# Second MLP of a fused attention, MLP, MLP kernel: three passes of four feature blocks in place of three sweeps over all twelve

## The chip, the cores and the metric

The kernel runs on one core of a Trainium2 chip. The metric is the device time of one execution in microseconds (us). Engines are named as in the profile: PE is TensorE (PEld its weight loads), DVE is VectorE, ACT is ScalarE, POOL is GpSimd, SP is SyncE, which here issues every DMA from one queue, in order.

## What is computed

Three stages follow each other: windowed attention on four batches of 576 tokens and eight heads, a first MLP that takes the maximum of three projections, and a second, gated MLP. The change touches the third alone. Cut to what matters:

```python
# second MLP: x is 2304 x 512, w_gate and w_val 512 x 1536, w_out 1536 x 512
g = x @ w_gate
silu = g * (1.0 / (1.0 + np.exp(-g)))
val = x @ w_val
out = (silu * val @ w_out).astype(np.float32)
```

## The kernel before

**Precision.** The weights arrive as 64-bit floats, which the chip reads as pairs of 32-bit integers. `single` (L91) turns such a pair into one float: a scaled copy on ACT (L96) and three integer instructions on DVE (L99, L100, L102). Every operand of a product is then split into a rounded head and a rest by `split` (L106): the head is an ACT copy (L107), the rest a subtraction (`low`, L85) on the engine that the caller names. A product is three matmuls: head by head, head by rest, rest by head.

**Tiles of the second MLP.** Tokens go in PAIRS = 3 pairs of blocks of HT = 384 tokens, called c. Features go in NF2 = 12 blocks of 128, called f. For each (c, f) the gate and value products of the pair of token blocks are computed together by a seven-product scheme (`PRODUCTS`, L31) in the manner of Strassen and Winograd: seven products of one combination of token blocks (A11, S2, A12, S3, S1, A22, S4) with one combination of weights (B11, T2, B21, T3, T1, T4, B22), where a plain computation takes eight. Each product is 2 x 3 matmuls of 384 columns.

**Preparing the weights of a block.** `prep(f)` (L510) has four pieces: `first` and `second_` load the gate and value weights, convert them with `single` and split them; `mixed` forms T1 to T4 by four DVE subtractions (L534) and splits the two tiles; `down_w` does the same to the rows of `w_out`. The rests of these five splits are on POOL. Every finished tile is also stored to `w_dram` (`store`, L507).

**The loops.** One step n is one (c, f), f inner: all 12 blocks for token pair 0, then for pair 1, then for pair 2. For c = 0 the weights are made by `prep`, AHEAD = 4 blocks ahead of their use; for c = 1 and 2 they are read back from `w_dram` by `load_w` (L553), five DMAs a block. The weight tiles live in two sets of buffers: 18 for the up side (tag "w"), 6 for the down side (tag "wo"). Token tiles are made by `tokens_steps(c)` (L590): four loads from `y_dram`, where the first MLP left its output, sums on DVE (L587), and 14 tiles split by ACT and DVE. They have 14 buffers, and for c = 1 and 2 four tiles use free weight buffers.

**A step.** `head(n)` (L636) issues products 1 and 6 of step n, and products 4 and 3 of step n - 1 with what follows them; `tail(n)` (L663) issues products 2, 7 and 5. ACT copies the first product (L641, the tile `s`) and takes two sigmoids (L653, L669); DVE does nine sums and products of 384 columns (L629, L657, L659, L660, L670). `act` (L631) rounds the two results on POOL (L88) and takes their rests on POOL (L85). The product accumulates in PSUM banks "a", "b" and "c", which DVE reads between products: PE can't go on to product 7 in bank "b" before DVE has read product 6 from it.

**The down product.** `down(c, g, t)` (L681) multiplies GROUP = 3 feature blocks for 128 tokens t (six of these to a token pair): 9 matmuls of 512 columns. The first group of a pair is copied to an accumulator by ACT (L694), the other three groups are added to it by DVE (L629, `acc`); the last one is stored to `out`. These come LAG = 4 steps behind, two to a step, as filler between the products.

**Order.** The framework lists each engine's instructions in an order that it plans at build time; engines then run in order and wait on semaphores. The vector work of a step has a priority of 100 over the rest (`HIGH`). Before the loop, the token tiles of pair 0 and the weights of blocks 0 to 3 are made beside the end of the first MLP.

Of the kernel before, what the change touches and what calls it, by code (L numbers as in the profile page):

```python
# [8 lines left out]
F32 = mybir.dt.float32  # L9
# [26 lines left out]
GROUP, LAG, AHEAD = 3, 4, 4  # L36
# [18 lines left out]
def kernel(ctx: ExitStack, tc, q0, k0, q1, k1, qk0, qk1, vv, w123, wo1, wgv, wo2, out):  # L55
# [26 lines left out]
    w_dram = dram.tile([NF2, 5, P, 2, 512], F32, name="w_dram")  # L82
# [414 lines left out]
    def second(apool, raws2, ps_o):  # L497
# [3 lines left out]

        def weight_tile(name, out=False):
            if out:
                return down_tile(name)
            return up_tile(name)

        def store(f, i, n=512):  # L507
            nc.sync.dma_start(out=w_dram[f, i, :, :, :n], in_=ws[0, f][i][:, :, :n].bitcast(F32))

        def prep(f):  # L510

            t = ws[0, f] = {}
            sums, ab = {}, {}
# [5 lines left out]
            def first():  # L519
                load(0)  # L520
                t[0] = weight_tile(f"u{f}_0")
                split(t[0], ab[0], nc.gpsimd)
                store(f, 0)

            def second_():
                load(1)
                t[3] = weight_tile(f"u{f}_3")
                split(t[3][:, :, :256], ab[1][:, 256:], nc.gpsimd)
                store(f, 3, 256)

            def mixed():
                tt = raws2.tile([P, 2, 512], F32, tag="sum", name="tt", bufs=1)
                b11, b21, b12, b22 = ab[0][:, :256], ab[0][:, 256:], ab[1][:, :256], ab[1][:, 256:]
                low_ = lambda o, x, y: nc.vector.tensor_tensor(out=o, in0=x, in1=y, op=ALU.subtract)  # L534
                t1, t3, t2, t4 = tt[:, 0, :256], tt[:, 0, 256:], tt[:, 1, :256], tt[:, 1, 256:]
                low_(t1, b12, b11)
                low_(t3, b22, b12)
                low_(t2, b22, t1)
                low_(t4, b21, t2)
                for i in (1, 2):  # L540
                    t[i] = weight_tile(f"u{f}_{i}")
                    split(t[i], tt[:, i - 1], nc.gpsimd)
                    store(f, i)

            def down_w():
                load(2)
                t[4] = weight_tile(f"u{f}_4", out=True)
                split(t[4], ab[2], nc.gpsimd)
                store(f, 4)

            return [first, second_, mixed, down_w]
# [16 lines left out]
        def tokens(c, name):  # L568

            x = raw_y[name]  # L570
            parts = blocks[c, name] = []
            for k in range(2):
                if (c, name) in {(1, "A11"), (1, "S2"), (2, "A12"), (2, "S3")}:
                    t = wpool.tile([P, 2, HT], F32R, tag="w", name="ya", bufs=3 * NF1)
# [15 lines left out]
        def tokens_steps(c):  # L590
# [7 lines left out]
            def four():  # L598
# [3 lines left out]
            rest = [lambda n=n: tokens(c, n) for n in ("S3", "S1", "A22", "S4")]  # L602
            return [lambda: load_y(c), one, lambda: tokens(c, "S2"), four] + rest

        def product(n, m, bank, first):

            c, f = divmod(n, NF2)
# [8 lines left out]
            w = ws[c, f][i]  # L616
            for k in range(2):
                y = blocks[c, a][k]
                wh, wl = [w[:, x, col + k * P:col + k * P + P] for x in range(2)]
# [5 lines left out]
        def scratch(tag):  # L625
            return temp.tile([P, HT], F32, tag=tag, name=tag)
# [3 lines left out]

        def act(n, i, h):  # L631
            t = acts[n, i] = actp.tile([P, 2, HT], F32R, tag="act", name="act")
            pool_round(t[:, 0], h)
            low(nc.gpsimd, t[:, 1], h, t[:, 0])

        def head(n):  # L636
            if n < PAIRS * NF2:
                p1 = product(n, 1, "a", True)
                with tc.high_priority(HIGH):
                    s1 = scratch("s1")  # L640
                    nc.scalar.copy(s1, p1)  # L641
                p6 = product(n, 6, "b", True)
                with tc.high_priority(HIGH):
                    u2 = scratch("u2")
                    add(u2, p6, s1)
                late[n] = s1, u2
            if n:
                s1, u2, u3, h0 = late.pop(n - 1)
                p4 = product(n - 1, 4, "b", False)
                with tc.high_priority(HIGH):  # L650
                    add(s1, p4, s1)
                    h1 = scratch("h1")
                    nc.scalar.activation(out=h1, in_=s1, func=AF.Sigmoid)  # L653
                p3 = product(n - 1, 3, "c", False)
                with tc.high_priority(HIGH):
                    add(u2, p3, u2)
                    nc.vector.tensor_tensor(out=h0, in0=h0, in1=u2, op=ALU.mult)  # L657
                    act(n - 1, 0, h0)
                    nc.vector.tensor_tensor(out=h1, in0=s1, in1=h1, op=ALU.mult)  # L659
                    nc.vector.tensor_tensor(out=h1, in0=u3, in1=h1, op=ALU.mult)  # L660
                    act(n - 1, 1, h1)

        def tail(n, piece):  # L663
# [3 lines left out]
            with tc.high_priority(HIGH):  # L667
                h0 = scratch("h0")
                nc.scalar.activation(out=h0, in_=p2, func=AF.Sigmoid)  # L669
                nc.vector.tensor_tensor(out=h0, in0=p2, in1=h0, op=ALU.mult)  # L670
            piece()
            p7 = product(n, 7, "b", False)
            with tc.high_priority(HIGH):
                u3 = scratch("u3")
# [6 lines left out]
        def down(c, g, t):  # L681

            po = ps_o.tile([P, 512], F32, tag="o", name="po", bufs=2)
            i, tt = divmod(t, HT // P)
            for f in range(g * GROUP, (g + 1) * GROUP):
                ah, al = [acts[c * NF2 + f, i][:, x, tt * P:tt * P + P] for x in range(2)]
                w = ws[c, f][4]
                nc.tensor.matmul(po, ah, w[:, 0], start=f == g * GROUP, stop=False)  # L688
                nc.tensor.matmul(po, ah, w[:, 1], start=False, stop=False)  # L689
                nc.tensor.matmul(po, al, w[:, 0], start=False, stop=f == (g + 1) * GROUP - 1)  # L690
            with tc.high_priority(HIGH):
                if g == 0:
                    acc[c, t] = accp.tile([P, 512], F32, tag="acc", name="acc")
                    nc.scalar.copy(acc[c, t], po)  # L694
                else:
                    add(acc[c, t], po, acc[c, t])
            if (g + 1) * GROUP == NF2:
                r0 = 2 * c * HT + t * P
                nc.sync.dma_start(out=out[r0:r0 + P, :], in_=acc.pop((c, t)))

        return prep, load_w, tokens_steps, head, tail, down


# [31 lines left out]
    apool = en("apool", 14, reuse_waits="tile")  # L735
    ps_o = en("ps_o", space=PSUM, reuse_waits="tile")
    prep, load_w, tokens_steps, head, tail, down = second(apool, raws2, ps_o)

    conv = tokens_steps(0) + [piece for f in range(AHEAD) for piece in prep(f)]
    spread(down_groups(*order[-2]) + up_groups(*order[-1]), conv[:16])  # L740
    spread(down_groups(*order[-1]), conv[16:])
    mctx.close()
    actp, accp, temp = em("actp", 10), em("accp", 7), em("temp", 2)
    ctx.enter_context(mctx)

    downs = []
    for n in range(PAIRS * NF2 + 1):
        c, f = divmod(n, NF2)
        others = []
        m = n + AHEAD  # L750
        if m < NF2:
# [85 lines left out]
```

## Time and profile before

| | before |
|---|---|
| median of 3 runs | 915.24 us (914.71 to 917.12) |
| the profiled execution, its own time | 913.06 us |
| its span, first to last instruction | 911.4 us |
| PE busy in the span | 867.0 us (95%) |
| DVE busy | 654.4 us (72%) |
| POOL busy | 484.1 us (53%) |
| ACT busy | 394.8 us (43%) |
| DMA queue of SP: packets' time as a share of 16 engines | 50.1% |

Shares of the whole span mix three stages with different limits. Matmuls are pipelined, so that their durations overlap: a busy PE says that it was never empty, and its rate is read from the distance between like instructions. The granted clock of PE is given as a share of its higher level.

### The profile page before, as it was taken

The numbers are of one execution on the slowest core, as the hardware profiler recorded it, in microseconds if no ns is written. First come the engines' busy times: TensorE is split into PE (matmuls) and PEld (weight loads), VectorE is DVE, ScalarE is ACT, GpSimd is POOL, SyncE is SP. The second block draws the span as 40 slices with busy tenths as digits, with TensorE's granted clock in tenths as the row PEclk, the third lists the DMA queues.
The fourth block names the chain that finished last, engine by engine and source line by source line (L and its number), as shares of the span: only waits on it lengthen the run. The fifth ranks groups of instructions, "written<-read, shape, count | busy, mean of one in ns | idle before, by whom it ended". The sixth has DMA issues, their size and how long they took to land.

```text
span 911.4 us, 16010 instructions
## 1 busy us (share of the span) xinstructions
PE 867.0 (95%) x5352; PEld 797.5 (88%) x5352; DVE 654.4 (72%) x1593; ACT 394.8 (43%) x1110; POOL 484.1 (53%) x675
## 2 busy tenths in 40 slices
PE   8999999999999999998787978899999999999997
PEld 5687889999999999998686867789999999999996
DVE  7998936676676757569699999999744566644553
ACT  6977658665575647243443433333121122121110
POOL 5586776767776675626547674752422231422221
PEclk9999999999999999999989999999999999999999
DMA  9842523233121411135786566789856673766401
GB/s 332 298 126 79 165 84 117 59 111 102 53 85 57 122 62 54 47 116 198 291 302 218 205 236 203 268 317 367 309 175 231 218 256 129 270 213 227 149 7 70
DMA packets 65138, 157.81 MB, mean 173 GB/s; under 512 B 6432, under 2 KB 26912, under 8 KB 65056
## 3 DMA queue, kind: packets, MB, share of 16 engines
q1 hardware_dynamic: 65056, 156.79, 50.1%
q8 instruction: 43, 0.70, 0.3%
q14 instruction: 39, 0.32, 0.1%
HBM read 119.01 MB, written 37.75 MB: 172 GB/s over the span
## 4 chain that ended last, share of the span: by engine, by line
PE 73%; DVE 17%; issue 3%; POOL 3%; DMA 3%; ACT 1%; SPq 0%; DVEq 0%; POOLq 0%; ACTq 0%
PE ps L124 10%; PE ps L122 10%; PE ps L123 10%; PE pg L620 5%; PE pg L622 5%; PE pg L621 5%; PE po L690 4%; PE po L688 4%; PE po L689 4%; DVE wf L100 3%; DVE wr L102 3%; DVE tt L534 3%; PE pv L400 2%; DMA wr<-wgv 2%; PE pc L620 2%
## 5 line engine op out<-in xcount | busy, mean ns | idle before, releaser
L122 PE MATMUL ps<-x,w 128*128 128x320 f32 (+1 forms) x576 | 172.0, 302 | 1.3 <-DVE m L165 1.0
L124 PE MATMUL ps<-x,w 128*128 128x320 f32 (+1 forms) x576 | 172.1, 300 | 0.1
L123 PE MATMUL ps<-x,w 128*128 128x320 f32 (+1 forms) x576 | 171.8, 299 | 0.0
L88 POOL TENSOR_SCALAR act<-h 128x384 fp32r<-128x384 f32 x72 | 45.3, 635 | 208.7 <-DVE h L657 201.0
L620 PE MATMUL pg<-ya,u 128*128 128x384 f32 x360 | 125.0, 349 | 20.6 <-DVE u L629 9.6
L621 PE MATMUL pg<-ya,u 128*128 128x384 f32 x360 | 123.2, 342 | 0.0
L622 PE MATMUL pg<-ya,u 128*128 128x384 f32 x360 | 123.1, 343 | 0.0
L122 PEld LDWEIGHTS ps<-x,w 128*128 128x128 f32 x576 | 107.9, 188 | 4.2 <-DVE m L165 1.3
L124 PEld LDWEIGHTS ps<-x,w 128*128 128x128 f32 x576 | 108.5, 188 | 2.6 <-DVE w L85 1.1
L123 PEld LDWEIGHTS ps<-x,w 128*128 128x128 f32 x576 | 108.5, 188 | 1.2 <-issue 0.9
L372 POOL TENSOR_SCALAR_AFFINE_SELECT t<-pk 128x512 fp32r<-128x512 f32 (+3 forms) x128 | 76.4, 619 | 49.9 <-PE pv L400 26.0
L620 PEld LDWEIGHTS pg<-ya,u 128*128 128x128 f32 x360 | 69.2, 192 | 31.7 <-DVE u L629 13.5
L688 PE MATMUL po<-u,act 128*128 128x512 f32 x216 | 86.9, 402 | 0.5 <-DVE acc L629 0.5
L689 PE MATMUL po<-u,act 128*128 128x512 f32 x216 | 86.3, 399 | 0.0
L690 PE MATMUL po<-u,act 128*128 128x512 f32 x216 | 85.5, 400 | 0.5 <-POOL act L85 0.5
L85 POOL TENSOR_TENSOR act<-h,act 128x384 fp32r<-128x384 f32 x72 | 82.3, 1150 | 3.2
L621 PEld LDWEIGHTS pg<-ya,u 128*128 128x128 f32 x360 | 69.3, 192 | 3.5
L324 ACT ACTIVATE z<-z,mn 128x128 f32<-128x128 f32 (+1 forms) x160 | 63.4, 398 | 20.3 <-DVE mn L319 19.4
L622 PEld LDWEIGHTS pg<-ya,u 128*128 128x128 f32 x360 | 69.2, 192 | 1.1 <-POOL u L85 0.8
L629 DVE TENSOR_TENSOR u<-pg,s 128x384 f32<-128x384 f32 x72 | 39.4, 551 | 41.8 <-PE pg L622 41.8
L85 POOL TENSOR_TENSOR u<-wr,u 128x512 fp32r<-128x512 f32 (+1 forms) x36 | 47.1, 1312 | 37.4 <-ACT u L107 37.4
L165 DVE TENSOR_TENSOR m<-ps,m 128x256 f32<-128x256 f32 (+1 forms) x96 | 43.2, 452 | 30.4 <-PE ps L124 27.1
(116 smaller groups left out, 2197.9 us busy)
## 6 DMA issues: line engine op xcount, KB each, us to landing
u<-w_dram SPq DMA_DIRECT2D x96, 512.0 KB, 5.3
w_dram<-u SPq DMA_DIRECT2D x48, 512.0 KB, 5.5
wr<-wgv SPq DMA_DIRECT2D x24, 512.0 KB, 5.2
qkr<-qk SPq DMA_DIRECT2D x24, 416.0 KB, 3.6
wr<-w SPq DMA_DIRECT2D x18, 512.0 KB, 6.0
wr<-wo SPq DMA_DIRECT2D x12, 512.0 KB, 5.9
u<-w_dram SPq DMA_DIRECT2D x24, 256.0 KB, 4.3
yr<-y_dram SPq DMA_DIRECT2D x12, 384.0 KB, 3.8
```

The costliest lines, as they stand in the source:

```text
L85: eng.tensor_tensor(out=out, in0=raw, in1=head.bitcast(F32), op=ALU.subtract)
L122: nc.tensor.matmul(ps, wh, xt_h, start=first, stop=False)
L123: nc.tensor.matmul(ps, wh, xt_l, start=False, stop=False)
L124: nc.tensor.matmul(ps, wl, xt_h, start=False, stop=last)
L324: nc.scalar.activation(out=z[:m, a], in_=z[:m, a], func=AF.Exp, scale=-1.0, bias=mn[:m, a:a + 1], accum_out=sm[:m, a:a + 1],)
L372: nc.gpsimd.affine_select(out=t[:, i, :n, :, :m], in_=w[:, :n, :, :m], compare_op=op, fill=0.0, base=0, pattern=[[0, n], [0, 2], [-sign, m ...
L620: nc.tensor.matmul(o, wh, y[:, 0], start=first and k == 0, stop=False, skip_group_check=True)
L621: nc.tensor.matmul(o, wh, y[:, 1], start=False, stop=False, skip_group_check=True)
L622: nc.tensor.matmul(o, wl, y[:, 0], start=False, stop=k == 1, skip_group_check=True)
L688: nc.tensor.matmul(po, ah, w[:, 0], start=f == g * GROUP, stop=False)
L689: nc.tensor.matmul(po, ah, w[:, 1], start=False, stop=False)
L690: nc.tensor.matmul(po, al, w[:, 0], start=False, stop=f == (g + 1) * GROUP - 1)
```

## The change

The loops are turned: the 12 feature blocks go in NPASS = 3 passes of PASS = 4. In a pass all three token pairs are worked through with the pass's four blocks, so that each weight tile is made once and stays in SBUF; `w_dram`, `store` and `load_w` are gone. Pairs run 0, 1, 2, then 2, 1, 0, then 0, 1, 2. A run of four steps with one pair in one pass is a segment; there are nine.

What goes through DRAM instead: in pass 0 each split token tile is stored to `a_dram` when it is made (3 x 14 tiles of 384 KB), and in passes 1 and 2 `tokens_again` loads the 14 tiles at each change of the pair, four times in all. The partial outputs of passes 0 and 1 are stored to `o_dram` (18 tiles of 256 KB in each pass) and loaded again in passes 1 and 2. Token tiles have 14 + EXTRA = 17 buffers.

The rests of the up weights' splits move from POOL to DVE, so that of five only that of `outs` stays on POOL. The rounding in `act` moves from POOL to ACT. The values' half tile is shared by an even and an odd block, so that four blocks take 14 up tiles in place of 16.

The down product takes four blocks at once, in two halves of 6 matmuls, three halves to a step, one segment behind. Only passes 1 and 2 add on DVE: 36 times in place of 54. Of the weights of blocks 0 to 3 the last two pieces move into step 0; blocks 4 to 7 are made in steps 4 to 12 and blocks 8 to 11 in steps 16 to 24, three pieces a step.

```diff
-GROUP, LAG, AHEAD = 3, 4, 4
+PASS = 4
+NPASS = NF2 // PASS
+SEGMENTS = [(p, c) for p in range(NPASS) for c in (range(PAIRS) if p % 2 == 0 else range(PAIRS - 1, -1, -1))]
+EXTRA = 3
...
-    w_dram = dram.tile([NF2, 5, P, 2, 512], F32, name="w_dram")
+    a_dram = dram.tile([PAIRS, 14, P, 2 * HT], F32, name="a_dram")
+    o_dram = dram.tile([NT, DM], F32, name="o_dram")
...
-                split(t[0], ab[0], nc.gpsimd)
-                store(f, 0)
+                split(t[0], ab[0], nc.vector)
...
+                both = up_tile(f"u{f}_3") if f % 2 == 0 else ws[f - 1][5]
+                t[3], t[5] = both[:, :, f % 2 * 256:f % 2 * 256 + 256], both
+                split(t[3], ab[1][:, 256:], nc.vector)
...
-                    split(t[i], tt[:, i - 1], nc.gpsimd)
-                    store(f, i)
+                    t[i] = up_tile(f"u{f}_{i}")
+                    split(t[i], tt[:, i - 1], nc.vector)
...
-        def load_w(c, f):
-
-            t = ws[c, f] = {}
-            for i, n in ((0, 512), (2, 512), (1, 512), (3, 256), (4, 512)):
-                t[i] = weight_tile(f"u{f}_{i}", out=i == 4)
-                nc.sync.dma_start(out=t[i][:, :, :n].bitcast(F32), in_=w_dram[f, i, :, :, :n])
...
+                t = apool[made[0] % (14 + EXTRA) // 14].tile([P, 2, HT], F32R, tag="a", name="ya")
+                made[0] += 1
+                kept = a_dram[c, 2 * names.index(name) + k].rearrange("p (a n) -> p a n", a=2)
+                if load:
+                    nc.sync.dma_start(out=t.bitcast(F32), in_=kept)
                 else:
-                    t = apool.tile([P, 2, HT], F32R, tag="a", name="ya")
-                split(t, x[:, k], nc.vector)
+                    split(t, raw_y[name][:, k], nc.vector)
+                    nc.sync.dma_start(out=kept, in_=t.bitcast(F32))
...
-            pool_round(t[:, 0], h)
-            low(nc.gpsimd, t[:, 1], h, t[:, 0])
+            split(t, h, nc.gpsimd)
...
+            if half == 0:
+                ps["o"] = ps_o.tile([P, 512], F32, tag="o", name="po", bufs=2)
+                o = acc[t] = accp.tile([P, 512], F32, tag="acc", name="acc")
+                if p:
+                    nc.sync.dma_start(out=o, in_=o_dram[r0:r0 + P, :])
+            po = ps["o"]
+            for j in range(2 * half, 2 * half + 2):
+                ah, al = [acts[g * PASS + j, i][:, x, tt * P:tt * P + P] for x in range(2)]
+                w = ws[p * PASS + j][4]
...
+            if half:
+                o = acc.pop(t)
+                with tc.high_priority(HIGH):
+                    if p:
+                        add(o, po, o)
+                    else:
+                        nc.scalar.copy(o, po)
+                nc.sync.dma_start(out=(out if p == NPASS - 1 else o_dram)[r0:r0 + P, :], in_=o)
...
+        if p + 1 < NPASS:
+            for q, when in enumerate((4, 9, 10, 11)):
+                if at == when:
+                    conv += prep((p + 1) * PASS + q)
+        if j == 0:
+            ahead = []
+            if g + 1 < len(SEGMENTS) and SEGMENTS[g + 1][1] != c:
+                p1, c1 = SEGMENTS[g + 1]
+                ahead = tokens_steps(c1) if p1 == 0 else tokens_again(c1)
```

## Rows read from the trace of the kernel before

**Rows 1.** Table by stretch: length; busy PE, PEld, DVE, ACT, POOL (count); PEclk, DMA, GB/s.
```profile
443.80:454.50 10.70, 6.83 (x36) 6.19 (x36) 5.54 (x6) 5.18 (x10) 6.55 (x5) 1.00 0.99 368
454.50:500.60 46.10, 37.55 (x170) 32.81 (x170) 44.16 (x70) 20.32 (x37) 27.22 (x23) 0.89 0.73 261
500.60:552.80 52.20, 43.59 (x203) 38.11 (x204) 50.12 (x71) 21.49 (x41) 35.50 (x31) 0.94 0.63 223
552.80:614.70 61.90, 54.53 (x252) 47.26 (x251) 61.76 (x93) 20.88 (x40) 37.37 (x33) 0.94 0.76 265
614.70:657.40 42.70, 42.70 (x227) 40.14 (x226) 38.63 (x64) 11.75 (x27) 15.25 (x18) 1.00 0.92 337
657.40:888.40 231.00, 231.00 (x1201) 214.32 (x1200) 122.13 (x221) 41.67 (x82) 66.87 (x82) 1.00 0.55 190
888.40:911.40 23.00, 18.38 (x79) 14.00 (x77) 7.86 (x13) 0.53 (x1) 3.09 (x4) 1.00 0.19 69
```

**Rows 2.** Timeline of ACT: a step's first copy, of steps 0 and 1, 16, and 35.
```profile
454.54 0.84 ACT L641 COPY s<-pg 128x384 f32<-128x384 f32 x2
...
657.37 0.48 ACT L641 COPY s<-pg 128x384 f32<-128x384 f32 x1 [2.82 <-PE pg L622]
...
876.61 0.48 ACT L641 COPY s<-pg 128x384 f32<-128x384 f32 x1 [4.70 <-PE pg L622]
```

**Rows 3.** Waits from 448 to 600 us: us in total, times, longest.
```profile
PE pg L620 <- DVE u L629: 9.6, 6, 3.2
PE pc L620 <- DVE u L629: 8.2, 6, 2.5
```

**Rows 4.** DVE's groups by shape from 448 to 600 us: count | busy us, mean ns.
```profile
L102 DVE SCALAR_TENSOR_TENSOR wr<-wr,wf 128x512 int32<-128x512 int32 x27 | 27.5, 1019 | 0.5
L100 DVE SCALAR_TENSOR_TENSOR wf<-wr,wf 128x512 int32<-128x512 int32 x27 | 25.7, 951 | 0.2
L99 DVE TENSOR_SCALAR wf<-wf 128x512 int32<-128x512 int32 x27 | 18.0, 667 | 4.7 <-ACT wf L96 4.7
L534 DVE TENSOR_TENSOR tt<-wr,tt 128x256 f32<-128x256 f32 x18 | 13.6, 756 | 0.0
L534 DVE TENSOR_TENSOR tt<-wr 128x256 f32<-128x256 f32 x18 | 11.1, 655 | 0.0
```

**Rows 5.** Durations over the whole trace by line: least/median/most ns, first and last start.
```profile
L629 DVE TENSOR_TENSOR u<-pg,s x72: 539/550/560, 457.3 to 886.1; 128x384 f32<-128x384 f32 x72
L102 DVE SCALAR_TENSOR_TENSOR wr<-wr,wf x66: 404/684/1786, 14.6 to 601.7; 128x512 int32<-128x512 int32 x54, 128x256 int32<-128x256 int32 x12
L99 DVE TENSOR_SCALAR wf<-wf x66: 280/428/1532, 12.5 to 596.1; 128x512 int32<-128x512 int32 x54, 128x256 int32<-128x256 int32 x12
L85 DVE TENSOR_TENSOR w<-wr,w x18: 664/682/1216, 17.1 to 83.5; 128x512 fp32r<-128x512 f32 x18
L85 POOL TENSOR_TENSOR act<-h,act x72: 1002/1115/1588, 480.4 to 897.5; 128x384 fp32r<-128x384 f32 x72
```

**Rows 6.** Timelines of DVE and of POOL at one moment: start us, us.
```profile
498.92 1.62 DVE L659 TENSOR_TENSOR h<-s,h 128x384 f32<-128x384 f32 x1
500.46 0.54 DVE L629 TENSOR_TENSOR u<-pc,u 128x384 f32<-128x384 f32 x1
...
498.54 1.58 POOL L85 TENSOR_TENSOR u<-tt,u 128x512 fp32r<-128x512 f32 x1
```

**Rows 7.** POOL's groups by shape from 448 to 600 us: count | busy us, mean ns.
```profile
L85 POOL TENSOR_TENSOR u<-wr,u 128x512 fp32r<-128x512 f32 x19 | 28.5, 1503 | 16.3 <-ACT u L107 16.3
L85 POOL TENSOR_TENSOR u<-tt,u 128x512 fp32r<-128x512 f32 x18 | 25.2, 1402 | 19.6 <-ACT u L107 19.4
```

**Rows 8.** Waits of SP's DMA queue over the span: us in total, times, longest.
```profile
SPq L508 <- POOL u L85: 112.9, 45, 7.9
```

**Rows 9.** Table by stretch again, around the first change of token pair.
```profile
603.00:645.00 42.00, 42.00 (x221) 39.17 (x220) 40.74 (x65) 13.04 (x30) 17.15 (x17) 1.00 1.01 374
```

**Rows 10.** DMA issues: count, KB each, median us from issue to landing.
```profile
yr<-y_dram SPq DMA_DIRECT2D x12, 384.0 KB, 3.8
```

More of the change, by code (lines that the diff above doesn't have):

```diff
@@ L500, in second @@
         made = [0]
[L502 to L508, printed above, removed]
+        names = ("A11", "S2", "A12", "S3", "S1", "A22", "S4")
         def prep(f):
[L512 to L513 removed]
+            t = ws[f] = {}
+            ab = {}
             def load(i):
@@ L679, in tail, with down @@
             late[n] = s1, u2, u3, h0
-        def down(c, g, t):
-            po = ps_o.tile([P, 512], F32, tag="o", name="po", bufs=2)
+        def down(g, t, half):
+            p, c = SEGMENTS[g]
+            r0 = 2 * c * HT + t * P
             i, tt = divmod(t, HT // P)
[L685 to L688, printed above, removed]
-                nc.tensor.matmul(po, ah, w[:, 1], start=False, stop=False)
[L690 to L699, printed above, removed]
@@ L734 @@
     raws2 = en("raws2", RAWS, reuse_waits="tile")
-    apool = en("apool", 14, reuse_waits="tile")
+    apool = [en("apool", 14, reuse_waits="tile")]
     ps_o = en("ps_o", space=PSUM, reuse_waits="tile")
[L737 to L741, printed above, removed]
+    STEPS = [(c, p * PASS + j) for p, c in SEGMENTS for j in range(PASS)]
@@ L742 @@
+    prep, tokens_steps, tokens_again, head, middle, tail, down = second(apool, raws2, ps_o)
+    conv = tokens_steps(0) + [piece for f in range(PASS) for piece in prep(f)]
+    spread(down_groups(*order[-2]) + up_groups(*order[-1]), conv[:18])
+    spread(down_groups(*order[-1]), conv[18:22])
+    conv = conv[22:]
     mctx.close()
-    actp, accp, temp = em("actp", 10), em("accp", 7), em("temp", 2)
+    actp, accp, temp = em("actp", 10), em("accp", 4), em("temp")
+    apool.append(en("apool2", EXTRA, reuse_waits="tile"))
@@ L744 @@
     ctx.enter_context(mctx)
[L746 to L751, printed above, removed]
[L752 to L761 removed]
+    downs, ahead = [], []
@@ new lines @@
+    for n, (c, f) in enumerate(STEPS):
+        g, j = divmod(n, PASS)
+        p = SEGMENTS[g][0]
+        at = n - p * PASS * PAIRS
+        if p + 1 < NPASS:
[7 more added lines that the diff above has]
+                ahead = tokens_steps(c1) if p1 == 0 else tokens_again(c1)
+        others = [ahead.pop(0) for _ in range(min(1, len(ahead)))] if j else []
+        others += conv[:3]
+        conv = conv[3:]
+        other = lambda: others.pop(0)() if others else None
@@ L762 @@
         step = lambda: downs.pop(0)() if downs else None
-        other = lambda: others.pop(0)() if others else None
         head(n)
+        step()
+        if n:
+            middle(n - 1)
+        if j == 0 and g:
+            downs += [lambda g=g, t=t, h=h: down(g - 1, t, h) for t in range(6) for h in range(2)]
         other()
         step()
-        if n < PAIRS * NF2:
-            other()
-            tail(n, step)
+        other()
+        tail(n, step)
         while others:
             other()
-        if c + 1 < PAIRS and f == NF2 - 1:
-            for piece in ts[3:]:
+        if j == PASS - 1:
+            for piece in ahead:
@@ L774 @@
                 piece()
-    for cc, g in ((PAIRS - 1, NF2 // GROUP - 1),):
-        while downs:
-            downs.pop(0)()
-        if n - LAG < (PAIRS * NF2 - GROUP):
-            for t in range(6):
-                down(cc, g, t)
+    middle(n)
+    downs += [lambda t=t, h=h: down(g, t, h) for t in range(6) for h in range(2)]
+    for piece in downs:
+        piece()
 def kernel(**inputs):
```

107 lines of the change are left out of this document (47 added, 60 removed).

## The prediction, made before the change was run

> **What bounds the kernel now.** I read the table by stretch first. PE is busy 95% of the span, but this is not one limit. I cut the second MLP where steps 0, 4, 8, 12 and 16 make their first copy on ACT (those of steps 0, 16 and 35 are in [rows 2]). From step 16 on PE is never empty: 231.00 of 231.00 us, and 42.70 of 42.70 before that [rows 1]. Nineteen steps from 657.37 to 876.61 us [rows 2] are 11.54 us each, and that is PE's own work. The loss lies in token pair 0, where the weights are made. There PE idles 10.70 - 6.83 = 3.9 us before step 0, then 46.10 - 37.55 = 8.6, 52.20 - 43.59 = 8.6 and 61.90 - 54.53 = 7.4 us: 28.4 us. The clock adds to it: a mean of 0.89, 0.94 and 0.94 [rows 1] between the levels of 1.2 and 2.4 GHz costs 0.11 x 46.1 + 0.06 x 52.2 + 0.06 x 61.9 = 11.9 us. Together 40.3 us are lost there, and none from step 12 to step 36.
>
> Who takes them is DVE: busy 44.16 + 50.12 + 61.76 = 156.0 of 160.2 us in steps 0 to 11 [rows 1], while PE waits for its reads of the product banks [rows 3]. Making weights is most of this: five groups take 95.9 of 152 us [rows 4]. They should take less. Undisturbed, L100 and L102 take 0.68 us, L99 0.43, a subtraction of 512 columns 0.68 and of 384 columns 0.55 [rows 5], so about 0.42 at 256 columns (an estimate along these two). Then 54 x 0.68 + 27 x 0.43 + 36 x 0.42 = 63.5 us, and 95.9 is 1.51 times that. The excess comes from POOL: a DVE product of 0.55 us began at 498.92 beside a POOL subtraction that lasted to 500.12, and took 1.62 us; the PSUM-reading sum after it took 0.54 [rows 6], and its kind never exceeds 560 ns [rows 5]. POOL is busy 100.1 of these 160.2 us, 62% [rows 1].
>
> **The change part by part.** PE's work stays the same: the same products, the same number of down matmuls. After 454.5 us it is 37.55 + 43.59 + 54.53 - 11.9 + 42.70 + 231.00 + 18.38 = 415.9 us, and the last stretch has 4.6 us in which PE is empty [rows 1]. A kernel with step 0 where it is and no loss behind it would have a span of 454.5 + 415.9 + 4.6 = 875. To this I add what the new order loses.
>
> *Start (term -3).* The stores to `w_dram` go. They stand in SP's queue until POOL has made the tile, 112.9 us in 45 waits, up to 7.9 us [rows 8], and the weight loads of the next block stand behind them. Removed, the loads come earlier. In their place 14 token stores (5.5 MB) stand ahead of the first weight loads. At 374 GB/s [rows 9] they fill 15 us, from 396 to 411, and could delay the first block by about 5 us. DVE also takes four rests more for each block. So -6 to +5, and I take -3.
>
> *DVE's load in pass 0.* A step has nine operations of 0.55 us, three of them with both inputs in SBUF. A block undisturbed: 3 x (0.68 + 0.68 + 0.43) + 4 x 0.42 for the conversions and mixtures, and now 3 x 0.68 + 0.42 for the rests that come from POOL: 9.5 us. A token pair: 14 x 0.55 + 5 x 0.94 (768 columns, the same line continued) = 12.4 us. POOL loses the rests (mean 1.50 and 1.40 us [rows 7]) and the rounding. What stays is two rests of 1.12 us [rows 5] a step and one of 1.5 a block: 43 us over sixteen steps of 160 us, 27% in place of 62%. Scaled so, the excess on SBUF operations falls from 0.51 to 0.22: a step 5.3 us, a block 11.7, a token pair 15.1. That the excess follows POOL's share is my choice; the bounds are none and all of POOL's time.
>
> The Trainium skill (SBUF — State Buffer, section Who interferes with whom) says that a DVE instruction with two SBUF inputs and a GpSimd instruction that reads SBUF exclude each other, and that the second to issue blocks for all of the first. By that rule taken to its end DVE would lose all 43 us of POOL where I count some 22; half of the 21 between lies where DVE has no room, and the time would be near 910 instead of 899. The trace agrees on the kind of stop (1.62 us beside a running POOL instruction), not on its being met every time.
>
> *Steps 0 to 3 (term +12).* Nothing of the down product is ready, so PE has little. With 42 matmuls of 384 and 18 of 512 columns in 11.54 us, by columns, the products of a step are 7.35 us. Of step 0, 36 matmuls (6.3 us) are done before 454.5 [rows 1], so that step 4's first product could end some 23 us after it. DVE has 4 x 5.3, the rest of block 3 (two pieces are moved here; with what is left before them 7 us undisturbed, an estimate, x 1.22 = 8.5) and half of token pair 1 (7.5): 37 us. DVE is the bound and the excess is 14; starts overlap a little, and I take 12, clock included (4 to 20).
>
> *Steps 4 to 15 (term +5).* PE has 46.2 us a segment. DVE has 21.2 + 11.7 + 15 = 48 in segment 1, 21.2 + 7.5 + 26.3 = 55 in segment 2, 21.2 + 8.8 = 30 in segment 3; together 133 against 138.6. Pass 0 adds nothing on DVE for the down product. Blocks 5, 6 and 7 get their tiles as blocks 0, 1 and 2 are released, in steps 9 to 11, and are needed in steps 13 to 15, so that the overload of segment 2 can run into segment 3. PE stays full at a DVE share of 97%, 40.74 of 42 us [rows 9], once down matmuls lie between the products. So 0 to 12.
>
> *Steps 16 to 27 (term +3).* The same boundary with six additions a segment of 0.7 us: 21.2 + 26.3 + 4 = 52 in segment 5, 34 in segment 6. 0 to 8.
>
> *Token loads (term +2).* At four changes 14 tiles of 0.39 MB come from DRAM, three into spare buffers. A tile is released by its product in the last step of the segment and needed by the same product a step later, so that each has about 10 us, two tiles to a product, and the last is needed some 28 us after the first release. Eleven tiles are 4.3 MB, 11.6 us at 374 GB/s [rows 9], and one lands in 3.8 us [rows 10]. PE's own work covers that. Without the cover a change would cost 11.6 + 3.8 - 10 = 5 us; so 0 to 15 for four changes and what is queued behind them on SP.
>
> *Partial outputs and the end (term +1).* A load of 256 KB stands between the two halves of a down product, about 5 us of PE's work ahead of its addition. If it is late, DVE's addition holds the next step's reads. 0 to 5. The rounding on ACT lies on an engine that is busy 41.67 of 231 us [rows 1], and costs nothing as long as that holds; moved back onto the path of the last step it would cost half a microsecond.
>
> Sum: 875 - 3 + 12 + 5 + 3 + 2 + 1 = 895 us of span. The profiled execution is 1.7 us longer than its span (913.06 against 911.4), and the median of the runs 2.2 us above that (915.24): 898.9, so 899.
>
> **The rivals.** *Nothing lost in segment 0 (better).* If DVE and POOL meet less often than I count, and weights are ready earlier because no store stands in SP's queue, the terms are -6, +4 and about 2 for the rest: 875 and a time of 879. For it: DVE's average in pass 0 is under PE's. Against it: 37 us of DVE beside 23 of PE at the very start.
>
> *The loss follows the block (no change).* Before, 40.3 us were lost while eight blocks were made beside the steps, 5.0 us a block. The new order also makes eight blocks beside steps, only later, and both later token pairs are split in pass 0, where one was before. With the same price per block: 871.1 + 40.3 = 911.4, a time of 915. Against it: the blocks now have full down work between products, where PE stayed full at a DVE share of 97%.
>
> *SP's queue stops the segments (slower).* Token loads wait in one queue for releases by PE; the loads of partial outputs stand behind them; a late one stops an addition on DVE, behind it the reads of the product banks, behind these PE. A change without cover costs the 5 us above, and a partial output that lands 3.8 us late [rows 10] comes on top: 8.8 us, four times, in place of my 2: 899 - 2 + 35 = 932. It decides from 4.5 us a change, since 18 - 2 = 16 us bring back the time before. For it: SP waits often and long already [rows 8]. Against it: reloads of 512 KB ran at 374 GB/s with PE full [rows 9].
>
> **How the numbers follow.** The forecast has 0.50 (time from 890 to 911), the better rival 0.18, the rival of no change 0.15, the slower one 0.17. A measurement of this kernel tells about 0.3% from no change, 2.7 us. Of the rival of no change I count 0.07 as same, 0.04 as faster and 0.04 as slower; 0.01 of the forecast falls under same. So faster 0.71, same 0.08, slower 0.21. For 8 in 10 the range takes most of the better rival and reaches over the rival of no change into the slower one: 878 to 926.
>
> **What would show it.** Right: PE near full from step 4, DVE's groups of conversions near their undisturbed means, the loss confined to steps 0 to 3 with DVE at the top of the waits there; no PE wait on token tiles at the four changes. Wrong: PE empty in steps 9 to 16 or 21 to 28 with DVE full; PE waiting on DMA for `ya`; DVE additions waiting on DMA; step 0 later than 454.5.

## The result and the profile after

The changed kernel takes 879.14 us (median; 877.96 to 879.35) against 915.68 us on the same chip: a ratio of 0.9597, 95% interval 0.958 to 0.9614, so 36.5 us or 4.0% faster. The forecast was 899 us, 16 us faster. The direction was right and the time lies inside the stated range, at its lower end, but the gain is 2.2 times the one forecast. It falls almost exactly on what the prediction called the better rival (879), to which it gave 0.18. Only the number does: that rival stood on terms of -6, +4 and about 2, and the same terms came out at -8.1, +12.7 and -2.2 (the sum is taken apart below).

The page of the changed kernel: busy time of the engines, then the granted clock in 40 slices.

```profile
PE 851.1 (97%) x5352; PEld 789.0 (90%) x5352; DVE 621.5 (71%) x1623; ACT 425.7 (49%) x1182; POOL 374.3 (43%) x555
...
PEclk9999999999999999999999999999999999999999
```

The table by stretch of the changed kernel, columns as in [rows 1]. From 446.4 us on the cuts are at the first copies on ACT of steps 0, 4, 8, 12, 16, 20 and 24, and near the last step's end.

```profile
400.00:436.00 36.00, 36.00 (x248) 36.00 (x247) 29.36 (x57) 14.11 (x30) 8.92 (x12) 1.00 0.63 230
436.00:446.40 10.40, 9.24 (x57) 8.87 (x55) 8.66 (x14) 5.78 (x13) 3.13 (x2) 1.00 0.65 202
446.40:482.10 35.70, 29.54 (x152) 26.11 (x153) 34.16 (x66) 19.36 (x41) 8.27 (x6) 1.00 0.49 174
482.10:526.70 44.60, 41.91 (x217) 38.21 (x216) 39.13 (x70) 22.97 (x47) 10.11 (x9) 1.00 0.68 227
526.70:576.00 49.30, 49.30 (x256) 45.50 (x255) 46.50 (x92) 26.23 (x52) 13.33 (x9) 1.00 0.61 215
576.00:619.50 43.50, 42.87 (x222) 39.30 (x222) 31.12 (x60) 18.07 (x38) 12.49 (x12) 1.00 0.37 125
...
665.70:714.50 48.80, 47.72 (x247) 43.83 (x246) 37.47 (x69) 17.36 (x35) 7.73 (x7) 1.00 0.49 165
...
852.00:877.40 25.40, 20.01 (x86) 15.38 (x84) 7.26 (x12) 1.51 (x3) 1.98 (x2) 0.95 0.29 104
```

Where [rows 1] showed PE empty for 28.4 us between 443.8 and 614.7 us, it is now empty for 1.2 + 6.2 + 2.7 + 0.0 + 0.6 us up to step 16, and for 1.1 us in the second boundary (steps 20 to 23). The granted clock stays at 1.00 up to the tail, with no gap of PE in steps 0 to 35 longer than 2.4 us: the 11.9 us that the lower level cost are gone as well. Only steps 0 to 3 look like the kernel before: DVE busy 34.16 of 35.70 us, PE 29.54.

What the prediction turned on is how far DVE's instructions are stretched. These are DVE's groups of weight preparation in steps 0 to 11 of the changed kernel (count | busy us, mean ns); they answer to [rows 4].

```profile
L104 DVE SCALAR_TENSOR_TENSOR wf<-wr,wf 128x512 int32<-128x512 int32 x16 | 11.8, 735 | 0.0
L106 DVE SCALAR_TENSOR_TENSOR wr<-wr,wf 128x512 int32<-128x512 int32 x16 | 11.6, 723 | 0.1
L103 DVE TENSOR_SCALAR wf<-wf 128x512 int32<-128x512 int32 x17 | 8.1, 479 | 4.7 <-ACT wf L100 4.7
L530 DVE TENSOR_TENSOR tt<-wr 128x256 f32<-128x256 f32 x10 | 5.0, 535 | 0.0
L530 DVE TENSOR_TENSOR tt<-wr,tt 128x256 f32<-128x256 f32 x10 | 4.3, 428 | 0.0
```

Undisturbed they would take 32 x 0.68 + 17 x 0.43 + 20 x 0.42 = 37.5 us; they took 40.8 by these rounded sums, 41.1 by count and mean: a factor of 1.10. This factor, the time of the five groups over their undisturbed time, is used throughout. Before, it was 1.51 (448 to 600 us). The prediction had put it at 1.22.

What is left of PE's waits in the second MLP, in total us, times, longest:

```profile
PE pc L611 <- DVE u L620: 3.7, 3, 2.4
...
PE pg L611 <- ACT s L634: 2.5, 2, 1.6
...
PE pg L611 <- DVE s L620: 1.6, 2, 1.5
...
PE pg L612 <- DVE ya L89: 0.7, 1, 0.7
```

No wait of PE on a DMA is among them, although the token tiles took longer to land than the 3.8 us of [rows 10]. Issues, KB each and median us to landing in the changed kernel:

```profile
ya<-a_dram SPq DMA_DIRECT2D x56, 384.0 KB, 5.6
...
acc<-o_dram SPq DMA_DIRECT2D x36, 256.0 KB, 2.6
```

### The profile page after: what moved, and what is told of

It is laid out like the page before. It is cut to its first block, busy times and chain, and to the rows that moved or that the text cites. A ratio compares the mean times of both kernels' runs of the same rounds, so it can differ in the third digit from the quotient of the medians.

```text
span 877.4 us, 15850 instructions
## 1 busy us (share of the span) xinstructions
PE 851.1 (97%) x5352; PEld 789.0 (90%) x5352; DVE 621.5 (71%) x1623; ACT 425.7 (49%) x1182; POOL 374.3 (43%) x555
## 4 chain that ended last, share of the span: by engine, by line
PE 73%; DVE 12%; DMA 9%; ACT 2%; issue 2%; POOL 1%; SPq 1%; DVEq 0%; ACTq 0%; POOLq 0%
PE ps L128 11%; PE ps L126 11%; PE ps L127 11%; DMA wr<-wgv 5%; PE pg L611 4%; PE pg L613 4%; PE pg L612 4%; PE po L690 4%; PE po L692 4%; PE po L691 4%; PE pv L404 2%; PE pt L360 2%; PE pc L611 2%; PE pc L613 2%; PE pc L612 2%
## 5 line engine op out<-in xcount | busy, mean ns | idle before, releaser
L89 POOL TENSOR_TENSOR act<-h,act 128x384 fp32r<-128x384 f32 x72 | 78.8, 1114 | 295.0 <-ACT act L111 259.6
L611 PE MATMUL pg<-ya,u 128*128 128x384 f32 x360 | 122.4, 340 | 6.5 <-ACT s L634 2.5
L612 PE MATMUL pg<-ya,u 128*128 128x384 f32 x360 | 121.1, 336 | 0.7 <-DVE ya L89 0.7
L613 PE MATMUL pg<-ya,u 128*128 128x384 f32 x360 | 120.6, 337 | 0.0
L690 PE MATMUL po<-u,act 128*128 128x512 f32 x216 | 85.9, 398 | 1.4 <-ACT act L111 0.7
L691 PE MATMUL po<-u,act 128*128 128x512 f32 x216 | 85.2, 394 | 0.0
L692 PE MATMUL po<-u,act 128*128 128x512 f32 x216 | 84.5, 396 | 0.0
L611 PEld LDWEIGHTS pg<-ya,u 128*128 128x128 f32 x360 | 67.6, 188 | 14.2 <-ACT s L634 3.1
L612 PEld LDWEIGHTS pg<-ya,u 128*128 128x128 f32 x360 | 67.6, 188 | 5.0 <-DVE ya L89 1.1
L613 PEld LDWEIGHTS pg<-ya,u 128*128 128x128 f32 x360 | 67.5, 188 | 0.4
L620 DVE TENSOR_TENSOR u<-pg,s 128x384 f32<-128x384 f32 x72 | 38.9, 551 | 35.9 <-PE pg L613 35.7
L100 ACT ACTIVATE wf<-wr 128x512 f32<-128x512 f32 (+1 forms) x66 | 41.5, 630 | 47.0 <-DMA wr<-wgv 33.5
L648 ACT ACTIVATE h<-s 128x384 f32<-128x384 f32 x36 | 18.9, 525 | 90.3 <-DVE s L620 88.7
```

The lines of the kernel that those rows point to most:

```text
L89: eng.tensor_tensor(out=out, in0=raw, in1=head.bitcast(F32), op=ALU.subtract)
L611: nc.tensor.matmul(o, wh, y[:, 0], start=first and k == 0, stop=False, skip_group_check=True)
L612: nc.tensor.matmul(o, wh, y[:, 1], start=False, stop=False, skip_group_check=True)
L613: nc.tensor.matmul(o, wl, y[:, 0], start=False, stop=k == 1, skip_group_check=True)
L690: nc.tensor.matmul(po, ah, w[:, 0], start=j == 0, stop=False)
L692: nc.tensor.matmul(po, al, w[:, 0], start=False, stop=j == PASS - 1)
```

## Experiments

Three theories stood against each other. P: the forecast put too high a price on how much POOL stretches DVE's instructions. O: the order of the passes carries the gain, and POOL hardly matters. Q: the stores to `w_dram` in SP's queue were the hidden cost. Ratios are to the kernel before on the same chip, with 95% intervals.

**The rests of the up weights back on POOL.**

```diff
-                split(t[0], ab[0], nc.vector)
+                split(t[0], ab[0], nc.gpsimd)
...
-                split(t[3], ab[1][:, 256:], nc.vector)
+                split(t[3], ab[1][:, 256:], nc.gpsimd)
...
-                    split(t[i], tt[:, i - 1], nc.vector)
+                    split(t[i], tt[:, i - 1], nc.gpsimd)
```

> The changed kernel (879.1 us) with the rests of the up weights' splits back on POOL, four of a block's five. Theory P (what was over-priced is the stop of DVE by POOL: it falls faster than POOL's share): POOL gains some 5.2 us a block (rests of 1.50, 1.40, 1.40 and 0.91 us in the trace of before), DVE loses 2.45, but its SBUF operations stretch again; the blocks of steps 4 to 12 and 16 to 24 and the start get longer, 886 to 895 us. Theory O (the order of the passes carries the gain, with down matmuls between the products from step 4 on and blocks spread over 24 steps; POOL hardly matters): within 4 us of 879. Theory Q (the stores in SP's queue were the cost): 879.

Measured: 895.97 us, ratio 0.9778 (0.9761 to 0.9794). 17 us come back from one choice of engine, a microsecond more than P's range; O and Q had 879. Its stretch of steps 0 to 11, and two of DVE's groups there:

```profile
454.50:589.00 134.50, 123.89 (x616) 111.16 (x616) 125.13 (x206) 69.30 (x139) 59.08 (x45) 0.97 0.57 196
...
L104 DVE SCALAR_TENSOR_TENSOR wf<-wr,wf 128x512 int32<-128x512 int32 x16 | 14.9, 933 | 0.0
L106 DVE SCALAR_TENSOR_TENSOR wr<-wr,wf 128x512 int32<-128x512 int32 x15 | 12.3, 821 | 0.0
```

DVE runs 20 instructions fewer than in the changed kernel and is busy 5 us longer. The factor of the five groups is 1.44. The step-0 copy comes at 454.5 us, as before the change, and steps 4 to 15 take 144.8 us against 137.4.

**The rounding back on POOL.**

```diff
-            split(t, h, nc.gpsimd)
+            pool_round(t[:, 0], h)
+            low(nc.gpsimd, t[:, 1], h, t[:, 0])
```

> The changed kernel with the rounding of the gated product back on POOL in place of ACT (0.64 us twice a step). Theory P: POOL's share in pass 0 goes from 26% to some 37%, and 2 to 6 us come back: 881 to 885. Theories O and Q: 879, within 2 us.

Measured: 878.71 us, ratio 0.9594 (0.9579 to 0.9608), no difference. P's 881 to 885 is missed, and the 879 of O and Q holds for this part. POOL is at 35% in steps 0 to 11 and the factor at 1.13. This part of the change is worth nothing by itself.

**Both back on POOL.**

> The changed kernel with both back on POOL, the rests of the up weights and the rounding: POOL's work as before, the new order of passes kept. Theory P: POOL is near 60% busy in pass 0 again and most of the 20 us by which the forecast was too high come back: 890 to 903, and DVE's L104 and L106 groups have means near 0.95 us again in place of 0.77 and 0.72. Theory O: under 885.

Measured: 902.09 us, ratio 0.9842 (0.9821 to 0.9863); POOL 49% (near 60 was expected), means of 966 and 972 ns, a factor of 1.56:

```profile
L106 DVE SCALAR_TENSOR_TENSOR wr<-wr,wf 128x512 int32<-128x512 int32 x16 | 15.6, 972 | 0.0
L104 DVE SCALAR_TENSOR_TENSOR wf<-wr,wf 128x512 int32<-128x512 int32 x16 | 15.5, 966 | 0.1
```

P's expectation of the time holds, and O's (under 885) falls. With the weight rests on POOL the rounding does cost: 6 us on top of the first experiment.

**The stores of the weight tiles put back.**

```diff
+        def store(f, i, n=512):
+            nc.sync.dma_start(out=w_dram[f, i, :, :, :n], in_=ws[f][i][:, :, :n].bitcast(F32))
...
                 split(t[0], ab[0], nc.vector)
+                store(f, 0)
```

> The changed kernel with the stores of every finished weight tile to a DRAM tensor put back on SP's queue, behind each split, as in the kernel before; nothing reads them. Theory Q (weight loads that stand behind such stores made the start late and held the blocks up): the first copy of step 0 moves from 446.4 us back toward 454.5, and the time is 887 to 895. Theories P and O: the stores wait for DVE and not for POOL now, and loads have slack: within 3 us of 879.

Measured: 886.79 us, ratio 0.9685 (0.9671 to 0.97). That is a shade under Q's range, and the whole loss lies at the start: the first copy comes at 457.4 us in place of 446.4, while from there to the end it takes 428.7 us against 431.0. P's and O's "within 3 us of 879" falls. The timelines of SP, ACT and PE, and the stretch between the two first copies, show how (line numbers of this kernel are one to eight higher):

```profile
444.15 0.32 SPq L509 DMA_DIRECT2D w_dram<-u  x1
444.52 0.42 SPq L136 DMA_DIRECT2D wr<-wo  x1
...
448.49 0.69 SPq L198 DMA_DIRECT2D y_dram<-y  x1
...
452.77 0.66 ACT L101 ACTIVATE wf<-wr 128x512 f32<-128x512 f32 x1 [2.15 <-DMA wr<-wo]
...
457.37 0.86 ACT L642 COPY s<-pg 128x384 f32<-128x384 f32 x2 [0.72 <-DMA y_dram<-y]
...
457.90 0.69 PE L619 MATMUL pg<-ya,u 128*128 128x384 f32 x1 [9.80 <-ACT s L642]
458.39 0.52 PE L620 MATMUL pg<-ya,u 128*128 128x384 f32 x1
...
446.40:457.40 11.00, 1.70 (x10) 1.38 (x8) 7.32 (x14) 3.56 (x7) 1.24 (x1) 0.77 1.00 338
```

PE ran out of work at 448.1 us, needed this copy to go on, and was empty for 9.8 us. The store at 444.15 us had waited 3.6 us for a rest on POOL, and the weight load behind it went out at 444.52, in the changed kernel at 440.45. The DMA engines were full with the stores (share 1.00): loads issued between 444 and 452 us took 8.2 to 9.3 us to land, those between 440 and 447 us in the changed kernel 3.5 to 6.5.

Two things then held the copy, and they ended almost together. Five of ACT's instructions on weight blocks stood between the last narrow one (128x256) and the copy in the planned order, two in the changed kernel; they waited for loads and for DVE and were done at 456.6 us. And the copy's own last wait, 0.72 us in its line above, is for the landing of the first MLP's last store (`y_dram<-y`): issued at 448.49, it took 8.8 us, in the changed kernel 3.1. So by this trace the copy would have come no earlier without the conversions ahead of it, and 0.7 us earlier without this landing: PE's 9.8 us can't be put on the order on ACT alone. In the changed kernel the same wait of PE is 1.64 us:

```profile
445.80 0.67 ACT L100 ACTIVATE wf<-wr 128x512 f32<-128x512 f32 x1
446.36 0.47 ACT L634 COPY s<-pg 128x384 f32<-128x384 f32 x1
...
446.88 0.45 PE L611 MATMUL pg<-ya,u 128*128 128x384 f32 x1 [1.64 <-ACT s L634]
```

**The kernel before with the rests on DVE, and with both moves.** The same lines as above are edited the other way round in the kernel before; its order, stores and reloads stay.

> The kernel before (915.7 us) with one part of the change alone: the rests of the up weights' splits on DVE in place of POOL. DVE gets 2.45 us a block more, POOL 5.2 less. Theory P: the five conversion groups, 95.9 us in 448 to 600 us, fall toward their undisturbed 63.5, which is more than the 22 us that nine blocks of rests add; 900 to 910 us. Theory O: DVE is full there and gets more work: 916 to 925.

Measured: 906.01 us, ratio 0.9899 (0.9882 to 0.9917). Giving the fuller engine more work made the kernel 9.3 us faster; the factor fell to 1.17, at a POOL share of 43%. Of these 65.6 us on POOL 23.5 are rounding (L88), which reads one tensor; the rest are subtractions (L85), which read two:

```profile
L85 POOL TENSOR_TENSOR act<-h,act 128x384 fp32r<-128x384 f32 x22 | 30.3, 1392 | 0.6
L88 POOL TENSOR_SCALAR act<-h 128x384 fp32r<-128x384 f32 x22 | 23.5, 1077 | 61.9 <-DVE h L657 58.6 <-DVE h L660 3.3
```

> The kernel before with the two moves alone: rests of the up weights on DVE, rounding of the gated product on ACT; order, stores and reloads as before. Theory P: most of the gain without the passes, 890 to 902. Theory O: 912 or more, the passes are needed. What is missing from here to 879 is the price of the order and of the stores.

Measured: 902.68 us, ratio 0.9862 (0.9845 to 0.9878). That is just above P's range and far under O's: a third of the gain is there without the order.

**The order alone.** POOL's work as before and the stores put back in the changed kernel.

> The changed kernel with POOL's work as before (rests of the up weights and rounding) and with the stores of every finished weight tile on SP: what is left of the change is the order of the passes, the reloads and the halves of the down product. If the parts add up as measured one by one (23 us for the two moves, 7.7 us for the stores), 902 + 8 = 910, the order alone is worth some 5 us. If the stores hurt more where they wait for POOL again, as they did before (112.9 us of waits), the order alone is worth nothing: 913 to 920. If the order alone carries gain that the stores hide in the kernel before, 903 or less.

Measured: 902.6 us, ratio 0.9869 (0.9855 to 0.9882). The order is worth 12.4 us, more than the 5 that a sum of the parts would leave, and about as much as with the stores left out (902.09; the two ratios' intervals overlap). So the stores show their 7.7 us only where the rests have left POOL. With POOL as before the first copy is late in any case: 453.2 us without the stores, 460.9 with them, and half of the later start is made up behind it (443.6 us from there to the end against 439.9).

**Another load on POOL.** A second, identical rest of the gated product, so that POOL's share rises without touching the weights.

```diff
             split(t, h, nc.gpsimd)
+            low(nc.gpsimd, t[:, 1], h, t[:, 0])
```

> The changed kernel with each rest of the gated product computed twice on POOL (two more instructions of 1.15 us a step, the same values): POOL's share in steps 0 to 11 goes from 24% to about 41 to 45%, as with the weight rests on POOL (44%), while the weights' preparation is left alone. If the stretching of DVE follows POOL's share, as the prediction scaled it, the five groups of the weight preparation go from 1.10 of their undisturbed time to 1.4 and the time to 890 or more. If it follows which instructions POOL runs beside the conversions (the rests of the same weights), they stay under 1.25 and the time under 884.

Measured: 892.16 us, ratio 0.9758 (0.9733 to 0.9783). Its stretch of steps 0 to 11, and the same two groups:

```profile
448.10:585.20 137.10, 125.43 (x630) 113.58 (x630) 132.57 (x224) 69.11 (x138) 58.03 (x44) 0.98 0.56 193
...
L104 DVE SCALAR_TENSOR_TENSOR wf<-wr,wf 128x512 int32<-128x512 int32 x16 | 14.0, 874 | 0.0
L106 DVE SCALAR_TENSOR_TENSOR wr<-wr,wf 128x512 int32<-128x512 int32 x16 | 13.3, 830 | 0.1
```

The time is where the share's expectation had it (890 or more), the factor lies between the two: POOL is at 42%, the factor is 1.28, where the share alone asked for 1.4 and the kind of instruction for less than 1.25. Steps 4 to 15 take 144.8 us, as with the weight rests on POOL. Part of the 13 us is the longer way of the gated product through POOL itself, which this kernel doubles: in these steps PE waits 1.3 us for POOL's `act`, and in the changed kernel not at all. How large the whole part is, the run doesn't tell.

**Smaller questions.**

> The changed kernel with one spare token buffer in place of three (EXTRA = 1), so that at a change of the pair 13 of 14 tiles wait for a release. The prediction held that PE's own work covers the loads with about 10 us of slack a tile: 879 to 881. Rival: the cover is thin, each of the four loaded changes and the two made ones costs 2 to 5 us more: 890 or more, PE waiting on DMA for the token tiles.

Measured: 881.49 us, ratio 0.963 (0.9616 to 0.9644), half a microsecond above the expected 879 to 881 and 2.4 us over the changed kernel, the intervals of the two ratios just apart. There is no wait of PE on the token tiles' DMA. The cover for the loads holds with one spare buffer.

> The changed kernel with the rests of every second token tile of pairs 1 and 2 on POOL in place of DVE (7 of 14 a pair, about 1.15 us on POOL against 0.63 on DVE). Theory P: POOL is 23% busy in steps 0 to 3 and DVE full there (34.16 of 35.70 us), so that relief and stretching about cancel: 877 to 882. If DVE's own instruction time were all that counts in steps 0 to 3, up to 4 us come off: 875.

Measured: 879.77 us, ratio 0.9607 (0.9593 to 0.9622), as expected if relief and stretching cancel; the factor rose to 1.17.

> The changed kernel with the last rest of a weight block, that of the down rows, on DVE in place of POOL as well (0.68 us against 1.71). Theory P as the runs so far have it (the stretching of DVE falls faster than POOL's share: 0.54 at 63%, 0.32 at 44%, 0.09 at 24%): little is left to gain, 878 to 880. Faster than 877 would say that POOL's 1.5 to 1.7 us instructions beside conversions are the costly ones, whatever their share.

Measured: 879.55 us, ratio 0.9609 (0.9593 to 0.9625), with a factor of 1.07. Nothing is left to gain here. (Over steps 0 to 11 the excesses that the expectation names as 0.54 and 0.32 are 0.50 and 0.44.)

> The changed kernel with the four pieces of weight block 3 in step 0 in place of two of them: the first copies of steps 0 and 1 stood on ACT behind a conversion copy that waits for a weight load, and PE lost 1.64 us there. If that queue position is what costs, the first copy comes at 444 to 446 us and up to 2 us are gained: 877 to 879. If DVE in steps 0 to 3 is the limit (34.16 of 35.70 us), block 3 in step 0 adds 5 us of work there: 881 to 884.

```diff
-    spread(down_groups(*order[-2]) + up_groups(*order[-1]), conv[:18])
-    spread(down_groups(*order[-1]), conv[18:22])
-    conv = conv[22:]
+    spread(down_groups(*order[-2]) + up_groups(*order[-1]), conv[:16])
+    spread(down_groups(*order[-1]), conv[16:20])
+    conv = conv[20:]
```

Measured: 876.65 us (875.98 to 877.54), ratio 0.9582 (0.9569 to 0.9595), the lowest of all. The reason given was wrong: PE's wait for the first copy is 1.66 us as it was, and the copy comes at 448.5. The other expectation, 5 us more of DVE's work in steps 0 to 3, did not come true either: DVE is busy for 32.79 us there, less than the 34.16 of the changed kernel. Steps 0 to 7 are 74.2 us long in place of 80.3; of these 6.1 us the later copy takes 2.1 back and steps 8 to 15 another 2.8. The interval overlaps the changed kernel's (0.958 to 0.9614), so that a gain is not shown.

## Why the prediction was off

The sum, term by term. The forecast's pieces add up to 895 us of span, the changed kernel's to 877.4.

| part | forecast us | measured us |
|---|---|---|
| first copy of step 0 | 451.5 (454.5 - 3) | 446.4 |
| steps 0 to 3 | 35.0 (23 + 12) | 35.7 |
| steps 4 to 15 | 143.6 (138.6 + 5) | 137.4 |
| steps 16 to 27 | 144.5 (138.5 + 3 + 2 + 1) | 140.1 |
| step 28 to the end | 120.4 | 117.8 |

The last row had no term; its 120.4 us are what the 875 of the sum leave for it, and why 2.6 us fewer were needed stays open.

**Right: what bounds the kernel.** DVE, stretched by POOL, held PE up while the weights were made. Taking rests off POOL at DVE's cost speeds up even the old order by 9 us (906.0 against 915.3), and putting them back costs the new order 17. PE's own work is as counted: from step 4 to the tail it is empty for 4.4 us in all.

**Right: steps 0 to 3.** 35.7 against 35 us, with DVE full. The prediction's largest loss is the one that came. That the size agrees so well is in part luck: DVE had 34.16 us of work and not 37, and PE was busy for 29.54 us and not 23.

**Wrong: the stretching of DVE.** The step that failed reads "Scaled so, the excess on SBUF operations falls from 0.51 to 0.22". It scaled the excess with POOL's share, 62% to 27%. The share was forecast well (24%; the forecast's own pieces make the sixteen steps 178.6 us and not 160, which is 24% too), but the excess of the five groups came out at 0.10. The table is worked out from the same five groups, over steps 0 to 11 of each kernel. The third column is POOL's share without the rounding. The fifth counts the DVE instructions of the groups that begin while a POOL subtraction is running, out of all of them; the sixth is what each of these lost on the mean.

| kernel | POOL's share | subtractions alone | factor | begun beside one | us lost in each |
|---|---|---|---|---|---|
| before | 62% | 53% | 1.50 | 43 of 114 | 0.67 |
| order alone | 51% | 41% | 1.37 | 22 of 65 | 0.57 |
| both back on POOL | 49% | 40% | 1.56 | 29 of 69 | 0.71 |
| weight rests back on POOL | 44% | 44% | 1.44 | 25 of 68 | 0.65 |
| before, weight rests on DVE | 43% | 28% | 1.17 | 24 of 111 | 0.40 |
| act rest twice | 42% | 42% | 1.28 | 25 of 68 | 0.43 |
| token rests on POOL | 38% | 38% | 1.17 | 15 of 68 | 0.42 |
| rounding back on POOL | 35% | 25% | 1.13 | 10 of 69 | 0.40 |
| before, both moves | 29% | 29% | 1.19 | 24 of 111 | 0.50 |
| changed, block 3 later | 25% | 25% | 1.09 | 13 of 77 | 0.31 |
| changed | 24% | 24% | 1.10 | 15 of 69 | 0.26 |
| changed, stores back | 24% | 24% | 1.11 | 10 of 65 | 0.40 |
| changed, last rest on DVE | 19% | 19% | 1.07 | 8 of 71 | 0.36 |

The last two columns hold nearly the whole excess: 28.8 of 31.1 us in the kernel before, and all of the 3.6 us in the changed one. In the thirteen kernels together, 263 instructions begin while a POOL subtraction is running and take 1.97 times their undisturbed time. The 96 during which one begins take 1.07, the 37 that meet only a rounding 1.07, and the 629 that meet nothing 0.99. So DVE is stopped one instruction at a time. From before to changed both factors of the loss fell: fewer were stopped, 22% in place of 38%, and a stop cost 0.26 us in place of 0.67. The scaling by a share allows for the first alone. Why the stops of the changed kernel are the shortest of all stays open.

The four kernels with weight rests on POOL have the four highest factors and the four longest stops (0.57 to 0.71 us). The row of the act rest done twice has as many stops as the weight rests, 25 of 68, but shorter ones, and a factor of 1.28 against 1.44. The rests of the weights are of one chain with the conversions: a rest starts when DVE and ACT have just finished its input, and DVE goes on to the next conversion of the same block. That the chain aligns the two engines so that the stops are long is argued, not shown. The Trainium skill (SBUF — State Buffer, section Who interferes with whom) puts it that "Issue order, not op shape, decides who blocks." The trace agrees: 1.97 where POOL's subtraction began first, 1.07 where DVE's instruction did. The other rule weighed in the prediction, every microsecond of POOL stopping DVE, would have given about 910; the measured 879 is far from it.

The term of steps 4 to 15 goes with this size in the kernels with the new order. With factors up to 1.17 these steps take 136.8 to 137.5 us; with 1.37, 1.28, 1.44 and 1.56 they take 142.6, 144.8, 144.8 and 148.9. The forecast had 143.6. PE's waits on DVE in them are 2.5 us in the changed kernel, 4.8 with the weight rests back on POOL and 8.5 with both back.

**Wrong: the start.** The term of -3, which came out at -8.1, saw the stores in SP's queue [rows 8], but priced only the weight loads behind them. It missed that the first copy of step 0 hangs on this queue in two ways, as the run with the stores put back shows: conversions that wait for weight loads stand ahead of it on ACT, and it waits itself for the landing of the first MLP's last store. Both parts of the change were needed: the first copy comes at 446.4 us only with the stores gone and the rests on DVE, and at 454.5 or 457.4 with either one put back. The prediction also looked for losses from 443.8 us on only. It left out the end of the first MLP, where blocks are made too. The kernel before, columns as in [rows 1]:

```profile
400.00:436.00 36.00, 33.12 (x223) 32.35 (x221) 32.78 (x53) 14.78 (x30) 18.50 (x19) 1.00 0.62 217
```

PE is empty for 2.9 us there, beside a POOL that is busy for 18.50; in the changed kernel it is full, beside one of 8.92. From 400 us to the first copy PE is empty for 7.6 us in the kernel before, for 6.0 with the weight rests back on POOL and for 1.2 in the changed one: 6.4 of the 8.1 us that the copy comes earlier.

**Too dear: loads and boundaries.** The terms of +3, +2 and +1 for steps 16 to 27 stood for 6 us, and these steps took 1.6 us over PE's own 138.5. Loads that land in 5.6 us instead of the 3.8 of [rows 10] were still hidden, with about 10 us of slack a tile as reckoned, and hold with one spare buffer. The slower rival, SP's queue stopping the segments, has nothing to stand on: in the second MLP PE never waits on a DMA. Against the rival of no change, that eight blocks cost 5 us each wherever they are made, speaks the order alone (12.4 us faster with POOL's work and the stores as before).

The whole gain of 36 us is thus: 12.4 us for the order with its reloads and halves (915 to 902.6), 15.8 us for the two moves off POOL within it (902.6 to 886.8), 7.7 us for the stores (886.8 to 879.1). Taken in another sequence the parts differ: the moves give 12.7 us in the old order, and the stores show nothing with POOL's work as before. How much of the 12.4 is due to down work between the products from step 4 on, how much to blocks spread over 24 steps, and how much to the 18 additions fewer on DVE, stays open; it wasn't tried.

## What to carry to other kernels

When a full engine's instructions are far over their undisturbed time beside another engine, moving work onto the full engine can make it faster: compare the stretch that goes with the instruction that comes. Don't scale such a stretch by the other engine's busy share. Count in the trace how many of the full engine's instructions begin while an instruction of the other that stops them is running, and what each of them loses; and take the undisturbed time as a rival's price. And price a queue by what waits for it on every engine: with the stores put back on SP, loads and stores took 8 to 9 us to land, a copy on ACT stood behind both, and PE was empty for 9.8 us.

## What the runs showed of the hardware

Of DVE's instructions that prepare weights, those that began while a POOL subtraction was running took 1.97 times their undisturbed time, and those that met nothing of POOL's 0.99. This holds also for the one that reads a single tensor (L99 before, L103 now): 0.95 us, 57 of them in the thirteen kernels, against 0.42. POOL's rounding beside a DVE busy 95% of the time cost nothing, though it took POOL's share from 24 to 35% (878.7 us); with the weight rests on POOL as well it cost 6 us (902.1 against 896.0). With rests of token tiles moved from DVE to POOL its subtractions took 38% at the same time (879.8 us); at 42 and 44%, with other rests, the time was 13 and 17 us longer.

Reloads of 22 MB of token tiles and 9.4 MB of partial outputs cost PE no wait; with them and their stores the kernel moved 130 MB through the DMA queues, the kernel before 158 MB. Gaps of up to 2.4 us in steps 0 to 8 left the granted clock at 1.00. In the kernel with the stores put back the gap of 9.8 us was followed by matmuls that took 0.52 us in place of 0.34, at a granted clock of 0.50 (457.4 to 462 us), which is the lower of the two levels, 1.2 GHz.
